# One more batch transposed by the DMA engines instead of TensorE, in an attention + ELU feed-forward kernel

## Chip, cores, metric

One core of one Trainium2 chip. The metric is device time in microseconds (us); a kernel is run several times, and what is told is the median of those runs with its lowest and highest. Every profile below is one execution of the kernel named. Its span is about 1.7 us shorter than the device time of the same run.

## The reference

Eight batches, eight heads, 576 positions, 64 numbers per head. Heads 0 to 3 see the last 32 positions (local), heads 4 to 7 see every 32nd position back (strided). The outputs become 4,608 tokens of 512 numbers, which go through two matrices with an ELU between them.

```python
scores = (1 / np.sqrt(D)) * np.matmul(q, k.transpose(0, 1, 3, 2))
rel = pos[:, None] - pos[None, :]
mask_local   = (rel >= 0) & (rel < 32)
mask_strided = (rel >= 0) & (pos[None, :] % 32 == pos[:, None] % 32)
attn = softmax(np.where(mask, scores, -1e9))
x = np.matmul(attn, v)                 # -> 4608 x 512
h = x @ w_in                           # -> 4608 x 2048   (layer 1)
g = np.where(h > 0, h, np.exp(np.minimum(h, 0)) - 1)
out = g @ w_out                        # -> 4608 x 512    (layer 2)
```

q, k and v are normal numbers times 0.1, so the scores are tiny and the softmax is nearly even over what the mask allows.

## The kernel before

TensorE multiplies nearly all of the time (busy 96% of the span). Layer 1 goes in tiles of 8 matmuls (128x256), layer 2 in steps of 4 (128x512), and the attention of later batches is fitted in between. Tokens go through in blocks of 256, which are numbered from 0.

The scores need q and k with the 64 numbers of a head on the partitions, so both are transposed after the load. There are two ways, and the kernel uses both. Batches 0, 1 and 2 use TensorE (`piece_T`), with a copy out of PSUM by VectorE or ScalarE; from batch 3 on, the DMA engines do it on their way from SBUF to SBUF (`dma_T`):

```python
    def dma_T(b, which):                       # issued by SP; 4 per batch
        i = b % 2
        out_, in_, n = {
            "qs": (qsT[i], qs.rearrange("p h c -> p (h c)"), RP),
            "ks": (ksT[i][:, 0:16 * RP], ks.rearrange("p h c -> p (h c)"), RP),
            ...                                # "ql", "kl": the local heads
        }[which]
        nc.sync.dma_start_transpose(out=out_.rearrange("p (c n) -> p c n", n=n), in_=in_)

    def piece_T(b, hp, engs=None, wide=True):
        ...
                nc.tensor.transpose(o, x, identity[0:n, 0:n])
        for i, (dst, blk) in enumerate(both):
            copy(engs[i] if engs else nc.vector, dst, ps[i])
```

There is one `qs` and one `ks` buffer for all batches, so the load of the next batch's strided q waits for the transpose of this one's. All loads from batch 1 on are issued by GpSimd, in the order of the program:

```python
    load_str(2, qs, q)                         # before the second attention loop
    load_str(2, ks, k)
    load_kl16(2)
    load_ql16(2)
    load_vl16(2)
    ...
    for it in ("2 S4 2 S5 2 2 B4 S6 2 E4 A5 S7 2 E5 B6 2 E6 A7 2 E7 v "
               "T0 2 S0 S1 2 T1 k B0 2 E0 S2 2 A1 E1 S3 2 B2 E2 2 A3 2 E3 t 2 x").split():
        # "2": a layer 2 step of blocks 0 and 1;  S, A/B, E: scores, value products, tail of batch 1
        # T: transposes of batch 1;  v: load of vs of batch 2;  k, x: loads of batch 3
        # t: piece_T of the strided heads of batch 2
    ...
    for p, n in ((0, 8), (1, 10)):             # the local heads of batch 2, between layer 1 tiles
        at(n, lambda p=p: do(("TT", 2, p)))
    for b in range(3, B):                      # st: the layer 1 tile of its first scores
        at(st - (3 if b == 3 else 4), lambda b=b: Ts(b))   # the four dma_T
    ...
        l2_to(n + 10)                          # layer 2 steps done before layer 1 tile n
```

The middle third of each value tile holds ones, so that one product gives a softmax sum along with the values; ScalarE writes them (`one_columns`), partly behind the first scores and partly after batch 0.

The softmax here doesn't subtract the row's maximum and nothing guards it: scores larger than these inputs give would overflow.

Of the kernel before, what the change touches and what calls it, by code (L numbers as in the profile page):

```python
# [17 lines left out]
D = 64  # L18
HG = 4
NS = 8  # L20
# [10 lines left out]
def kernel(  # L31
# [46 lines left out]
    qlb = [const([RP, 2, NS, 2 * D], BF16, f"qlb{i}") for i in range(2)]  # L78
    qld = [t.rearrange("p a s c -> p (a s c)").rearrange("p (h c) -> p h c", h=HG) for t in qlb]
    klb = [const([LQ, 2, LB, 2 * D], BF16, f"klb{i}") for i in range(2)]  # L80
# [32 lines left out]
    def load_ql16(b):  # L113
        if b < 3:
            nc.gpsimd.dma_start(out=qld[b % 2][0:RS],
                                in_=q[b, 0:HG].rearrange("h (p s) d -> p h (s d)", s=NS))
            return
        for h in range(HG):
            nc.gpsimd.dma_start(  # L119
                out=qlb[b % 2][0:RS, h // 2, :, (h % 2) * D:(h % 2 + 1) * D],  # L120
                in_=q[b, h].rearrange("(p s) d -> p s d", s=NS))
# [59 lines left out]
    dist = const([RS, RS], I32, "dist")  # L181
    nc.vector.memset(warm, 1.0)  # L182
    nc.vector.memset(identity, 1.0)
    nc.vector.memset(base_l, 1.0)
    for t in (qs, ks):
# [3 lines left out]
        base=0, pattern=[[1, 128]], channel_multiplier=-1,  # L189
    )  # L190
    load_str(0, qs, q)
    load_str(0, ks, k)
# [40 lines left out]
    def pitch(b):  # L233
        return RS if b < 3 else RP

    def t_parts(b, hp, nm):
        i, a, n = b % 2, hp % 2, RS
        if hp >= 2:
            src = qs if nm == "q" else ks
            dst = (qsT if nm == "q" else ksT)[i][:, a * 8 * n:(a + 1) * 8 * n]  # L240
            blk = [src[0:n, 2 * a + j // 4, (j % 4) * 128:(j % 4 + 1) * 128] for j in range(8)]
        elif nm == "q":
            dst = qlT[i][:, a * 8 * n:(a + 1) * 8 * n]
            blk = ([qlb[i][0:n, a, j] for j in range(NS)] if b not in (1, 2) else
                   [[qld[i][0:n, 2 * a + x, j * D:(j + 1) * D] for x in range(2)]
                    for j in range(NS)])
        else:
            dst = klT[i][:, PRE + a * S:PRE + (a + 1) * S]
            blk = [klb[i][:, a, j] for j in range(LB)]
        return dst, blk  # L250
# [4 lines left out]
    def piece_T(b, hp, engs=None, wide=True):  # L255
# [6 lines left out]
        for i, (dst, blk) in enumerate(both):  # L262
            n = S // len(blk)
            for j, x in enumerate(blk):
                o = ps[i][:, j * n:(j + 1) * n]
                if type(x) is list:
                    for z in range(2):
                        nc.tensor.transpose(o[z * D:(z + 1) * D], x[z], identity[0:n, 0:n])
                else:
                    nc.tensor.transpose(o, x, identity[0:n, 0:n])  # L270
        for i, (dst, blk) in enumerate(both):
# [252 lines left out]
    P = [(p, u) for p in range(4) for u in range(2)]  # L524
    def one_columns(i):
        for t in (vlx[i], vsx[i]):
            o = t.rearrange("p a t (y d) -> p (a t) y d", d=D)[:, :, 1, :]
            nc.scalar.copy(o, warm[0:o.shape[0], 0:D].unsqueeze(1).to_broadcast(o.shape))  # L528

    for it in ("f7 S0 S1 1 f6 T1 f6 S2 S3 m f8 T2 T3q T3k f3 S4 S5 f3 S6 S7 M4 f3 E4 M5 f3 E5 M6 f3 E6 "  # L530
               "v M7 f3 E7 M0 f3 E0 M1 f3 E1 M2 f3 E2 M3 f12 E3").split():
# [3 lines left out]
        elif it[0] == "f":  # L535
            spins(n)
        elif it == "1":
            one_columns(0)
        elif it == "v":
# [17 lines left out]
    nc.vector.memset(qlb[1][64:RP], 0.0)  # L557
    nc.vector.memset(vlx[1][0:PRE, :, 0, :], 0.0)
    one_columns(1)
    load_str(1, qs, q)  # L560
# [23 lines left out]
    load_str(2, ks, k)  # L584
    load_kl16(2)
    load_ql16(2)
    load_vl16(2)

# [12 lines left out]

    for it in ("2 S4 2 S5 2 2 B4 S6 2 E4 A5 S7 2 E5 B6 2 E6 A7 2 E7 v "
               "T0 2 S0 S1 2 T1 k B0 2 E0 S2 2 A1 E1 S3 2 B2 E2 2 A3 2 E3 t 2 x").split():
        n = int(it[-1]) if it[-1].isdigit() else 0
        if it == "2":
            l2_to(l2n[0] + 1)
        elif it == "v":
            load_str(2, vs, v)
        elif it == "k":
            load_kl16(3)  # L610
            load_ql16(3)
            load_vsx16(3)
        elif it == "t":
            for p in (2, 3):
                piece_T(2, p)
        elif it == "x":
            load_str(3, qs, q)
            load_str(3, ks, k)
            load_vl16(3)
        elif it[0] == "T":  # L620
            piece_T(1, n, (nc.vector, nc.scalar))
        elif it[0] in "AB":
# [8 lines left out]

    def Ts(b):
        for w in ("qs", "ks", "kl", "ql"):
            dma_T(b, w)


    SC = {2: (2.5, 5.5, 9, 12), }
    SC.update({b: tuple(15 + 16 * (b - 3) + 4 * i for i in range(4)) for b in range(3, B)})
    for p, n in ((0, 8), (1, 10)):
        at(n, lambda p=p: do(("TT", 2, p)))  # L640

    for b in range(3, B):
        st = int(SC[b][0])
        if b > 3:
            at(st - 13, lambda b=b: (load_str(b, qs, q), load_str(b, ks, k), load_kl16(b),
                                     load_ql16(b), load_vsx16(b), load_vl16(b)))
        at(st - (3 if b == 3 else 4), lambda b=b: Ts(b))
    for b in range(2, B):
# [7 lines left out]
    for n, (j, t) in enumerate(L1S):  # L656
        for f in jobs.pop(n, []):
            f()
        l2_to(n + 10)
        for f in jobs.pop(n + .5, []):  # L660
# [33 lines left out]
```

## Time and profile before

| | before |
|---|---|
| device time | 324.3 us (324.25 to 324.75, 3 runs); beside the changed kernel 324.52 (324.25 to 324.92, 4 runs) |
| profiled span | 322.6 us |
| TensorE busy | 310.8 us, 96% |
| mean granted clock of TensorE | 0.999 |

How to read a line of the timeline: start, length, engine, source line, operation, output<-input, shape, how many, and in brackets the idle time before it with what ended it. The main lines are shown in the prediction. Two more views: SP's and GpSimd's timelines around the first DMA transposes, those of batch 3, with the busy and DMA figures of that stretch (columns as in the prediction's stretches).

```profile
87.31 1.47 SPq L169 DMA_TRANSPOSE qsT<-qs  x1
88.89 1.88 SPq L169 DMA_TRANSPOSE ksT<-ks  x1
```

```profile
94.19 0.72 POOL L143 DMA_DIRECT2D ks<-in_k_dram  x1 [0.52 <-issue]
```

```profile
87.00:94.00 7.00, 7.00 (x67) 4.48 (x66) 4.69 (x10) 5.19 (x11) 0.75 (x1) 1.00 1.00 168
```

The lengths in SP's lines are SP's issuing, not the transfer: in the changed kernel SP's line for ksT of batch 2 ends at 62.94 us, and TensorE waits for that transpose until 68.56. The transfer shows in its user: the load of the next ks overwrites what the transpose reads, and goes at 94.19, 5.3 us after that transpose's issue, so the transpose took at most that. The DMA share (last column but one) is 1.00. (The DMA share adds up the times of all packets that start in the stretch and divides by the time of 16 engines; it comes out over 1 in places.)

### The profile page before, as it was taken

The numbers are of one execution on the slowest core, as the hardware profiler recorded it, in microseconds if no ns is written. First come the engines' busy times: TensorE is split into PE (matmuls) and PEld (weight loads), VectorE is DVE, ScalarE is ACT, GpSimd is POOL, SyncE is SP. The second block draws the span as 40 slices with busy tenths as digits, with TensorE's granted clock in tenths as the row PEclk, the third lists the DMA queues.
The fourth block names the chain that finished last, engine by engine and source line by source line (L and its number), as shares of the span: only waits on it lengthen the run. The fifth ranks groups of instructions, "written<-read, shape, count | busy, mean of one in ns | idle before, by whom it ended". The sixth has DMA issues, their size and how long they took to land.

```text
span 322.6 us, 7819 instructions
## 1 busy us (share of the span) xinstructions
PE 310.8 (96%) x2992; PEld 223.6 (69%) x2992; DVE 239.5 (74%) x485; ACT 220.2 (68%) x429; POOL 115.6 (36%) x162
## 2 busy tenths in 40 slices
PE   7898998989999999999999999999999999999994
PEld 5658953577667777777777777777777777777763
DVE  7664973477667888888888988898888866666660
ACT  3697766677688888777777777778888643443431
POOL 6352368788046903790259125920000000000000
PEclk9999999999999999999999999999999999999999
DMA  8999999999499949993999599969211111111112
GB/s 160 191 205 207 208 151 142 153 147 129 52 143 182 122 70 155 172 141 64 137 158 161 70 136 167 149 77 169 57 35 35 34 35 33 34 35 49 51 33 65
DMA packets 113990, 36.36 MB, mean 113 GB/s; under 512 B 101154, under 2 KB 107458, under 8 KB 113954
## 3 DMA queue, kind: packets, MB, share of 16 engines
q0 software_dynamic: 79696, 18.87, 61.3%
q1 hardware_dynamic: 32766, 16.28, 24.6%
q10 hardware_dynamic: 1492, 0.74, 1.0%
q8 instruction: 23, 0.38, 0.5%
q14 instruction: 13, 0.11, 0.1%
HBM read 38.04 MB, written 9.44 MB: 147 GB/s over the span
## 4 chain that ended last, share of the span: by engine, by line
PE 83%; DVE 6%; ACT 5%; DMA 3%; issue 1%; SPq 0%; DVEq 0%; ACTq 0%
PE ops L463 36%; PE hps L406 33%; PE sc L293 4%; PE ox L345 3%; DVE g L421 2%; DMA kl<-in_k_dram 2%; DMA ksT<-ks 1%; PE idle L487 1%; DVE g L440 1%; PE opl L478 1%; PE tp L270 1%; DVE he L420 1%; ACT vsx L528 1%; ACT big L437 1%; ACT e L296 1%
## 5 line engine op out<-in xcount | busy, mean ns | idle before, releaser
L463 PE MATMUL ops<-w_out_sb,g 128*128 128x512 bf16 x560 | 143.6, 380 | 0.1
L406 PE MATMUL hps<-xT,w_in_sb 128*128 128x256 bf16 x1088 | 140.7, 273 | 1.3 <-DVE g L421 1.3
L406 PEld LDWEIGHTS <-w_in_sb 128*128 128x128 bf16 x1088 | 117.3, 114 | 23.6 <-issue 1.5
L413 ACT ACTIVATE he<-hps 128x512 f32<-128x512 f32 x136 | 80.2, 593 | 52.3 <-PE hps L406 50.0
L421 DVE TENSOR_TENSOR g<-he,hps 128x512 bf16<-128x512 bf16 x130 | 89.4, 687 | 13.6
L463 PEld LDWEIGHTS <-g 128*128 128x128 bf16 x560 | 50.4, 98 | 37.2 <-DVE g L421 0.3
L420 DVE TENSOR_SCALAR he<-he 128x512 bf16<-128x512 f32 x130 | 57.7, 444 | 20.9 <-ACT he L413 19.5
L296 ACT ACTIVATE e<-sc 128x576 bf16<-128x576 f32 (+1 forms) x64 | 38.5, 645 | 4.6 <-PE sc L293 4.6
L468 ACT COPY osb<-ops 128x512 f32<-128x512 f32 x35 | 20.5, 587 | 12.3 <-PE ops L463 9.4
L143 POOL DMA_DIRECT2D qs<-in_q_dram x8 | 6.2, 774 | 48.9 <-DMA qsT<-qs 47.5
L348 ACT ACTIVATE ln<-ox 64x288 f32<-64x288 f32 x40 | 16.3, 409 | 10.7 <-PE ox L345 10.1
L125 POOL DMA_DIRECT2D klb<-in_k_dram x28 | 20.7, 747 | 7.9 <-DMA w_in_sb<-in_moe_w_in_dram 5.2
L133 POOL DMA_DIRECT2D vlx<-in_v_dram x28 | 21.9, 782 | 4.1 <-DMA w_out_sb<-in_moe_w_out_dram 1.9
L313 DVE TENSOR_TENSOR xT<-ox,rc 64x288 bf16<-64x288 f32 x40 | 18.1, 453 | 5.7 <-ACT rc L351 5.4
L317 DVE TENSOR_TENSOR xT<-ox,rc 64x288 bf16<-64x288 f32 x40 | 18.1, 453 | 5.5 <-ACT rc L351 5.1
L119 POOL DMA_DIRECT2D qlb<-in_q_dram x20 | 16.6, 833 | 13.8 <-DMA ks<-in_k_dram 10.0
L134 POOL DMA_DIRECT2D vlx<-in_v_dram x28 | 17.3, 618 | 4.2 <-DMA qlb<-in_q_dram 2.1
L351 ACT ACTIVATE rc<-ln 128x288 f32<-128x288 f32 x40 | 17.7, 443 | 1.3
L138 POOL DMA_DIRECT2D vsx<-in_v_dram x20 | 16.2, 816 | 0.9 <-DMA klb<-in_k_dram 0.9
L349 ACT ACTIVATE ln<-ox 64x288 f32<-64x288 f32 x40 | 16.1, 403 | 0.5
L304 DVE TENSOR_TENSOR pm<-e,mask_l 128x576 bf16<-128x576 bf16 x32 | 13.5, 453 | 3.3 <-ACT e L296 3.0
L487 PE MATMUL idle<-warm 128*128 128x256 bf16 x92 | 14.3, 299 | 1.3 <-DVE warm L182 1.3
(101 smaller groups left out, 243.2 us busy)
## 6 DMA issues: line engine op xcount, KB each, us to landing
out_dram<-osb SPq DMA_DIRECT2D x31, 144.0 KB
qs<-in_q_dram POOLq DMA_DIRECT2D x8, 288.0 KB, 6.4
ks<-in_k_dram POOLq DMA_DIRECT2D x8, 288.0 KB, 8.7
w_in_sb<-in_moe_w_in_dram POOLq DMA_DIRECT2D x2, 1024.0 KB, 17.0
w_out_sb<-in_moe_w_out_dram POOLq DMA_DIRECT2D x4, 512.0 KB, 15.7
klb<-in_k_dram POOLq DMA_DIRECT2D x28, 72.0 KB, 8.2
vlx<-in_v_dram POOLq DMA_DIRECT2D x28, 72.0 KB, 3.6
qlb<-in_q_dram POOLq DMA_DIRECT2D x20, 72.0 KB, 7.0
```

The source lines that it names most:

```text
L125: nc.gpsimd.dma_start(out=klb[b % 2][:, h // 2, :, (h % 2) * D:(h % 2 + 1) * D], in_=k[b, h].rearrange("(t p) d -> p t d", p=LQ))
L133: nc.gpsimd.dma_start(out=t[PRE:128], in_=x)
L296: nc.scalar.activation(e[0:R], sc[0:R, :, 0:W], ACT.Exp, scale=scale)
L313: nc.vector.tensor_mul(xs[:, u * W:(u + 1) * W], o[pr], rc[pr])
L317: nc.vector.tensor_mul(dst, o[pr].rearrange(pat, b=3, s=NS), rc[pr].rearrange(pat, b=3, s=NS))
L351: nc.scalar.activation(rc, ln, ACT.Exp, scale=-1.0)
L406: nc.tensor.matmul(hps[:, mm], lhsT=w_in_of(m, c), rhs=xT[:, c, r0:r0 + SUB], start=(c == 0), stop=(c == KC - 1))
L413: nc.scalar.activation(e, hps, ACT.Exp)
L420: eng.tensor_scalar(e1, e, scalar1=1.0, scalar2=1.0, op0=ALU.min, op1=ALU.subtract)
L421: nc.vector.tensor_tensor(gt, e1, hps, op=ALU.max)
L463: nc.tensor.matmul(ops, lhsT=g[:, m, kk * 128:(kk + 1) * 128], rhs=w_out_sb[:, m, :], start=(m == 0), stop=(m == MC - 1))
L468: nc.scalar.copy(o_sb, ops)
```

## The change

The intent: take the last transposes that TensorE can be spared (batch 2) off it, fill two idle places of TensorE with layer 2 steps, and take a hold-up of ScalarE and VectorE at 25 to 31 us away by writing the constants at the start. Its core:

```diff
@@ load_ql16: q of batches 1, 2 strided, like later batches @@
-        if b < 3:
-            nc.gpsimd.dma_start(out=qld[b % 2][0:RS],
-                                in_=q[b, 0:HG].rearrange("h (p s) d -> p h (s d)", s=NS))
-            return
@@ constants, right after the first memset @@
     nc.vector.memset(warm, 1.0)
+    nc.vector.memset(vlx[1][0:PRE, :, 0, :], 0.0)
...
+    for i in range(2):
+        one_columns(i)                 # was: behind the first scores, and after batch 0
@@ pitch @@
-        return RS if b < 3 else RP
+        return RS if b < 2 else RP
@@ second attention loop @@
-    for it in ("2 S4 2 S5 2 2 B4 S6 2 E4 A5 S7 2 E5 B6 2 E6 A7 2 E7 v "
-               "T0 2 S0 S1 2 T1 k B0 2 E0 S2 2 A1 E1 S3 2 B2 E2 2 A3 2 E3 t 2 x").split():
+    for it in ("2 S4 2 S5 2 2 B4 S6 2 E4 A5 S7 2 E5 B6 2 E6 A7 v 2 t E7 T0 2 S0 S1 2 T1 k B0 2 E0 S2 2 A1 E1 S3 t B2 2 "
+               "E2 A3 E3 x").split():
         elif it == "v":
             load_str(2, vs, v)
+            load_kl16(2)               # these three stood ahead of vs
+            load_ql16(2)
+            load_vl16(2)
         elif it == "k":
+            load_str(3, qs, q)         # these two stood at "x"
+            load_str(3, ks, k)
+            load_vsx16(3)
             load_kl16(3)
             load_ql16(3)
-            load_vsx16(3)
         elif it == "t":
-            for p in (2, 3):
-                piece_T(2, p)
+            Ts(2, *(("qs", "ks") if l2n[0] < 10 else ("kl", "ql")))
...
-    for p, n in ((0, 8), (1, 10)):
-        at(n, lambda p=p: do(("TT", 2, p)))
...
-        at(st - (3 if b == 3 else 4), lambda b=b: Ts(b))
+        at(st - 4, lambda b=b: Ts(b, "qs", "ks"))
+        at(st - (0 if b == 3 else 4), lambda b=b: Ts(b, "kl", "ql"))
...
-        l2_to(n + 10)
+        l2_to(max(n + 10, min(13 + (n + 2) // 2, 16)))
```

Left out: the strided branch of `piece_T` that q of batches 1 and 2 no longer needs, and piece T0's second copy, which goes from ScalarE to VectorE.

More of the change, by code (lines that the diff above doesn't have):

```diff
@@ L78 @@
     qlb = [const([RP, 2, NS, 2 * D], BF16, f"qlb{i}") for i in range(2)]
-    qld = [t.rearrange("p a s c -> p (a s c)").rearrange("p (h c) -> p h c", h=HG) for t in qlb]
     klb = [const([LQ, 2, LB, 2 * D], BF16, f"klb{i}") for i in range(2)]
@@ L190, with one_columns @@
     )
+    def one_columns(i):
+        for t in (vlx[i], vsx[i]):
+            o = t.rearrange("p a t (y d) -> p (a t) y d", d=D)[:, :, 1, :]
+            nc.scalar.copy(o, warm[0:o.shape[0], 0:D].unsqueeze(1).to_broadcast(o.shape))
+    for i in range(2):
+        one_columns(i)
     load_str(0, qs, q)
@@ L243, in t_parts @@
             dst = qlT[i][:, a * 8 * n:(a + 1) * 8 * n]
-            blk = ([qlb[i][0:n, a, j] for j in range(NS)] if b not in (1, 2) else
-                   [[qld[i][0:n, 2 * a + x, j * D:(j + 1) * D] for x in range(2)]
-                    for j in range(NS)])
+            blk = [qlb[i][0:n, a, j] for j in range(NS)]
         else:
@@ L265, in piece_T @@
                 o = ps[i][:, j * n:(j + 1) * n]
-                if type(x) is list:
-                    for z in range(2):
-                        nc.tensor.transpose(o[z * D:(z + 1) * D], x[z], identity[0:n, 0:n])
-                else:
-                    nc.tensor.transpose(o, x, identity[0:n, 0:n])
+                nc.tensor.transpose(o, x, identity[0:n, 0:n])
         for i, (dst, blk) in enumerate(both):
@@ L524 @@
     P = [(p, u) for p in range(4) for u in range(2)]
-    def one_columns(i):
-        for t in (vlx[i], vsx[i]):
-            o = t.rearrange("p a t (y d) -> p (a t) y d", d=D)[:, :, 1, :]
-            nc.scalar.copy(o, warm[0:o.shape[0], 0:D].unsqueeze(1).to_broadcast(o.shape))
-    for it in ("f7 S0 S1 1 f6 T1 f6 S2 S3 m f8 T2 T3q T3k f3 S4 S5 f3 S6 S7 M4 f3 E4 M5 f3 E5 M6 f3 E6 "
+    for it in ("f7 S0 S1 f6 T1 f6 S2 S3 m f8 T2 T3q T3k f3 S4 S5 f3 S6 S7 M4 f3 E4 M5 f3 E5 M6 f3 E6 "
                "v M7 f3 E7 M0 f3 E0 M1 f3 E1 M2 f3 E2 M3 f12 E3").split():
@@ L536 @@
             spins(n)
-        elif it == "1":
-            one_columns(0)
         elif it == "v":
@@ L557 @@
     nc.vector.memset(qlb[1][64:RP], 0.0)
-    nc.vector.memset(vlx[1][0:PRE, :, 0, :], 0.0)
-    one_columns(1)
     load_str(1, qs, q)
@@ L584 @@
     load_str(2, ks, k)
-    load_kl16(2)
-    load_ql16(2)
-    load_vl16(2)
     L2S = [(j, kk, part) for j in range(NSUB) for kk in range(2) for part in range(4)]
@@ L600, in l2_to, with Ts @@
             l2n[0] += 1
-    for it in ("2 S4 2 S5 2 2 B4 S6 2 E4 A5 S7 2 E5 B6 2 E6 A7 2 E7 v "
-               "T0 2 S0 S1 2 T1 k B0 2 E0 S2 2 A1 E1 S3 2 B2 E2 2 A3 2 E3 t 2 x").split():
+    def Ts(b, *names):
+        for w in names:
+            dma_T(b, w)
+    for it in ("2 S4 2 S5 2 2 B4 S6 2 E4 A5 S7 2 E5 B6 2 E6 A7 v 2 t E7 T0 2 S0 S1 2 T1 k B0 2 E0 S2 2 A1 E1 S3 t B2 2 "
+               "E2 A3 E3 x").split():
         n = int(it[-1]) if it[-1].isdigit() else 0
@@ L608 @@
             load_str(2, vs, v)
+            load_kl16(2)
+            load_ql16(2)
+            load_vl16(2)
         elif it == "k":
+            load_str(3, qs, q)
+            load_str(3, ks, k)
+            load_vsx16(3)
             load_kl16(3)
             load_ql16(3)
-            load_vsx16(3)
         elif it == "t":
-            for p in (2, 3):
-                piece_T(2, p)
+            Ts(2, *(("qs", "ks") if l2n[0] < 10 else ("kl", "ql")))
         elif it == "x":
-            load_str(3, qs, q)
-            load_str(3, ks, k)
             load_vl16(3)
         elif it[0] == "T":
-            piece_T(1, n, (nc.vector, nc.scalar))
+            piece_T(1, n, (nc.vector, nc.scalar if n else nc.vector))
         elif it[0] in "AB":
@@ L630, in at @@
         jobs.setdefault(int(2 * n) / 2, []).extend(its)
-    def Ts(b):
-        for w in ("qs", "ks", "kl", "ql"):
-            dma_T(b, w)
     SC = {2: (2.5, 5.5, 9, 12), }
     SC.update({b: tuple(15 + 16 * (b - 3) + 4 * i for i in range(4)) for b in range(3, B)})
-    for p, n in ((0, 8), (1, 10)):
-        at(n, lambda p=p: do(("TT", 2, p)))
     for b in range(3, B):
```

## The prediction

Passages that told of the hardware what no trace of this case shows are cut from the recorded text, and the places are marked. The 5.5 us and the 1.5 to 1.9 us for a transpose were read from the trace of the kernel before. The 0.1 us "for a switch of shape" is an estimate; in the chain of the kernel before a layer 2 step takes 0.97 us behind scores (at 81.49) and 0.86 behind a layer 1 tile (at 91.31). Both kernels give the DMA transposes 80 rows where 72 hold data (`RP` and `RS`).

> **What bounds the kernel now.** Names used below: qs and ks are the tiles of the strided heads' q and k, ql and kl of the local heads'; with T they are the transposed ones; a layer 2 step is four 128x512 matmuls into one accumulator. I read the page first, busy shares and slices, then TensorE's waits, then the chain of waits and TensorE's timeline where those waits lie.
>
> ```profile
> PE 310.8 (96%) x2992; PEld 223.6 (69%) x2992; DVE 239.5 (74%) x485; ACT 220.2 (68%) x429; POOL 115.6 (36%) x162
> ...
> PE   7898998989999999999999999999999999999994
> ...
> DMA  8999999999499949993999599969211111111112
> ...
> 0.00:20.00 20.00, 16.52 (x224) 11.85 (x224) 13.84 (x39) 12.12 (x21) 8.72 (x16) 1.00 1.02 180
> 20.00:40.00 20.00, 18.67 (x203) 16.60 (x203) 13.29 (x24) 15.04 (x25) 9.12 (x14) 1.00 1.14 209
> 40.00:60.00 20.00, 18.52 (x217) 9.79 (x216) 11.37 (x24) 13.18 (x26) 14.40 (x21) 1.00 1.48 157
> 60.00:80.00 20.00, 18.82 (x239) 13.30 (x238) 13.48 (x30) 15.24 (x32) 16.90 (x23) 1.00 1.45 134
> 80.00:100.00 20.00, 19.80 (x212) 13.33 (x211) 13.47 (x28) 14.77 (x29) 7.18 (x11) 1.00 0.85 110
> ```
>
> In the last five lines the columns are stretch, length, busy us of PE, PEld, DVE, ACT, POOL, clock, DMA share, GB/s. TensorE is the bound: from 80 us to the last slice it hardly idles. So a microsecond gained before 80 us moves the end by one, provided no new wait takes it back. Two things can be gained: TensorE work (3.0 us of transposes, below) and idle time, 1.3, 1.5 and 1.2 us in the second to fourth stretch (20 minus the first busy number). The 3.5 us in the first are the loads and latency at the start.
>
> Who causes the idle time:
>
> ```profile
> PE hps L406 <- DVE g L421: 1.3, 1, 1.3
> PE sc L293 <- ACT klT L253: 1.3, 1, 1.3
> ...
> PE so L368 <- DVE pm L298: 1.1, 1, 1.1
> ...
> ```
>
> The columns are total us, times, longest. The first lies at 31.2 us, the second at 53.7, the third at 70.8. The chain shows what is behind the first:
>
> ```profile
> 25.15 0.91 DVE qlb L557
> ...
> 27.14 1.04 ACT vsx L528
> 28.18 0.92 ACT big L437
> ...
> 30.04 1.23 DVE g L440
> ...
> 32.49 1.03 PE hps L406 x8
> ```
>
> A memset of 0.91 us on VectorE and one of 0.22 behind it hold back ScalarE's copies of ones into v's second buffers; behind those stands the first exponential of layer 1, whose matmuls were done at 26.7. VectorE starts 1.4 us late, and a TensorE buffer comes free late.
>
> [...] the first of batch 3 is issued at 87.31 us and the load it holds up goes at 92.92, with a DMA share of 0.2 just before; SP takes 1.5 to 1.9 us for each, so 80x2048 bf16 (0.33 MB) every 1.9 us is at most 172 GB/s. I use 5.5 us from issue to landing.
> [...] GpSimd stands 47.5 us in four waits on the transposes of qs. So the order in a queue decides when a transfer starts.
> [...] Here one record lasts 197 ns, but they are pipelined:
>
> ```profile
> 63.85 0.43 PE L270 MATMUL tp<-identity,qs 72*128 72x72 bf16 x8
> ...
> 64.77 0.42 PE L270 MATMUL tp<-identity,ks 72*128 72x72 bf16 x8
> 65.03 1.03 PE L463 MATMUL ops<-w_out_sb,g 128*128 128x512 bf16 x4
> ```
>
> 32 of them hold TensorE from 63.85 to 65.03, 1.18 us, 37 ns each.
>
> **The change part by part.**
> *Transposes of batch 2 off TensorE.* The strided pieces free 1.18 us. The two local ones begin at 78.44 and 83.62; each delays what follows by some 0.77 us (0.65 to the next group, and about 0.1 for a switch of shape). Sum 1.18 + 2 x 0.77 = 2.7 us on the bound engine, all of it path. VectorE loses 8 copies of 0.45 us; only the 0.2 us wait on klT at 81.19 is on the path.
> *Batch 1.* With q strided in the load, its two pieces need 8 transposes of 128 columns, not 16 of 64: 0.38 us becomes about 0.26, twice, 0.24 us. The k copy of piece 0 moves from ScalarE (0.64) to VectorE (0.45) and ends about 0.2 us earlier; that path sets the wait at 53.7.
> *Ones and a memset to the start.* The 1.3 us wait at 31.2 goes. The price: four copies on ScalarE, which back to back took 0.72 and 0.95 here, so 2 x 1.67 = 3.35 us; ScalarE is free from 2.08 (table load) to 6.07 (k lands). They fit with 0.6 us to spare. The 0.22 us memset stands in front of the memsets of qs and ks, which the first strided loads wait for: at most 0.2 us lost. Net gain 1.1 us.
> *Layer 2 steps moved.* The second attention loop has 13 rather than 16 steps; the other three come in the first five layer 1 tiles. Walking the timeline, 13 steps leave TensorE waiting before the last value product of batch 1 (pm 0.5 us late) and again before the first layer 1 tile of the next block: logarithm 0.41, exponential 0.44 and multiply 0.46, about 1.5 us with the handovers, less one step of 0.97, 0.6 us. Given back: the 1.05 us at 70.8 and some 0.35 in smaller gaps around it, now filled by steps. Net gain 0.3 us.
> *Loads.* q of batches 1 and 2 becomes 4 issues of 0.83 us for one of 0.74, some 2.6 us more of GpSimd each. The strided pieces drain well: k of batch 1, 576 runs each, landed at 43.5, 43.9, 44.4 and 44.8, while the contiguous q, 288 long runs, landed 2.0 us later. Since GpSimd keeps 8 DMAs in flight (its k issue at 29.89 goes as the weight load eight DMAs back lands, 10.1 + 19.5 = 29.6, and the next six go by the same rule), I place qs and ks of batch 2 at 49.1 and 49.9. Their latencies then:
>
> ```profile
> L143 POOL DMA_DIRECT2D ks<-in_k_dram x1: 722/722/722, 48.6 to 48.6; - x1
> DMA to landing us min/median/max: 6.3/6.3/6.3
> ```
>
> So ks lands at 56.2, SP takes 1.9 us, and 5 us after its issue, about 61, ksT is there. The first scores of batch 2 stand at 67.74 now and at about 65 after the gains. That is 4 us of room. kl and ql have over 8 us. Nothing on the path.
>
> Sum: 2.7 + 0.24 + 0.2 + 0.2 + 1.1 + 0.3 = 4.7 us; 324.3 - 4.7 = 319.6 us, 1.5% less.
>
> **The rivals.**
> *Transposes late.* If the crowded DMA engines (share 1.5 between 40 and 80 us[...]) stretch a transpose to 9 us or more, TensorE waits at the first scores of batch 2 and takes 1 to 3 us back: 320.5 to 322.5. For it: the change adds four transposes of over 1,200 packets each and 4,032 packets of q in the fullest stretch; ksT already held up scores twice, 0.7 us in total. Against it: the 4 us of room, and from 48 to 52 us the share is only 1.0, because GpSimd's issue and not the engines limits the flow. I give it 25%.
> *Batch 3 pushed back.* Its loads go out behind those of batch 2, its strided ones behind the transposes. In the kernel before they landed by 80 us for transposes at 87 to 93; now about 75 to 86. Its local transposes are moved three tiles later, and their use is 16 us on. Would cost 1 us; 10%.
> *The layer 2 shift buys nothing.* VectorE feeds both stretches; if filling the gap at 70.8 only reopens it before tile 0, the end is 320 or a little over; 25%. If instead pm comes in time, 319.
> *Start collides.* If ScalarE is late for the cast of k at 6.07, the whole start shifts by up to 1 us: 320.5; 10%.
> *More than counted.* If every gap between 40 and 80 us closes (2.7 us), the result is near 317.5. Against it: the wait before the scores at 53.7 hangs on ScalarE's eviction of layer 2 and VectorE's copies, which the change hardly touches.
>
> **Range and chances.** Transposes and the early wait (about 4 us) are nearly certain; the rest runs from -2.5 to +1.7. Predicted 319.6 us, 8 in 10 within 318.0 to 321.8. Over 2% faster means under 317.8, which needs the last rival: 0.08. Slower by 2% would need 11 us of new waits: 0.01. Within 2%: 0.91.
>
> **What would show it.** TensorE: no transposes after 60 us, 92 fewer in number. Its waits: no 1.3 us at layer 1 near 31 us; the wait on klT near 53 still over 0.8 us; the wait of 1.1 us on pm near 70 gone, and a new one of 0.3 to 0.8 us at the first layer 1 tile after batch 1. ScalarE's copies of ones done before 6.0 us. No wait of TensorE's weight loads on ksT<-ks before 80 us; if one over 0.5 us stands there, the first rival holds. The offset of the two timelines should be 1.1 to 1.4 us at the first layer 2 step, about 3.5 at the first layer 1 tile of block 2 (65.90 now; three layer 2 steps short), and 4.5 to 5 from 90 us on. If the offset shrinks again after 90 us, my claim that the rest is bound by TensorE alone is wrong.

## The result

The changed kernel took 325.64 us (325.28 to 326.29, 4 runs) against 324.52 us for the kernel before in the same rounds. The ratio is 1.0036, with a 95% interval of 1.0015 to 1.0056. Executions over 1.5% slower than the fastest of the same kernel are left out of the means. A ratio is always the mean time of one kernel's fast runs over the mean of the other's of the same rounds, so it is not quite the ratio of the medians. The class "within 2%" is right. The time is not: 319.6 was predicted, with 318.0 to 321.8 as the range, and 325.64 lies outside it. Not 1.5% was gained, but 0.4% lost.

Source lines differ by a few between the kernels: L290, L403, L460 here are L293, L406, L463 before. First the page of the changed kernel: busy shares, slices of TensorE, of its clock and of the DMA engines.

```profile
PE 306.6 (95%) x2856; PEld 222.2 (69%) x2900; DVE 237.8 (73%) x478; ACT 219.5 (68%) x428; POOL 120.2 (37%) x168
...
PE   7899998869999899999999999999999999999995
...
PEclk9999999979999999999999999999999999999998
DMA  7999999999999999993999599939211111111212
```

PEld has 2,900 records where before had 2,992: the 92 fewer that were predicted. But the ninth slice (64.8 to 72.9 us) has a 6 for TensorE and a 7 for its clock, and the DMA engines, which showed a 4 at 81 to 89 and at 113 to 121 us before, show a 9 there. TensorE's waits name the rest (total us, times, longest):

```profile
PE sc L290 <- DMA ksT<-ks: 3.1, 1, 3.1
PE sc L290 <- DVE klT L254: 1.4, 2, 1.0
...
PE sc L290 <- DMA qlT<-qlb: 1.0, 1, 1.0
...
PE so L371 <- DVE pm L301: 0.5, 1, 0.5
...
PE hps L403 <- DVE xT L314: 0.4, 1, 0.4
```

Against the three lines of the prediction: the 1.3 us on g and the 1.1 us on pm are gone, the wait on klT has stayed (1.0), and the two small ones foreseen are there (0.55 and 0.40 against 0.5 and 0.6). New are two waits on transposes. Where the first lies, in TensorE's timeline:

```profile
64.47 1.03 PE L460 MATMUL ops<-w_out_sb,g 128*128 128x512 bf16 x4
68.56 0.30 PE L290 MATMUL sc<-qsT,ksT 64*128 64x72 bf16 x8 [3.07 <-DMA ksT<-ks]
...
70.30 1.90 PE L403 MATMUL hps<-xT,w_in_sb 128*128 128x256 bf16 x8
```

TensorE is ready for the first scores of batch 2 at 65.5 us (the prediction said about 65) and starts them at 68.56. Two things are to be seen. Behind the wait, a layer 1 tile of 8 matmuls takes 1.90 us where such a tile takes 1.06; the stretches of 2 us say why. Their last columns are clock, DMA share and GB/s:

```profile
60.00:80.00 20.00, 15.48 (x156) 10.61 (x158) 10.82 (x22) 12.79 (x27) 12.43 (x18) 0.91 1.65 162
...
68.00:70.00 2.00, 1.44 (x19) 1.04 (x21) 0.41 (x1) 0.65 (x1) 1.36 (x3) 0.89 2.04 193
70.00:72.00 2.00, 2.00 (x17) 1.24 (x16) 1.26 (x4) 1.13 (x2) 1.85 (x3) 0.50 1.42 117
72.00:74.00 2.00, 1.74 (x20) 0.98 (x21) 0.92 (x2) 1.74 (x4) 2.00 (x4) 0.75 1.90 194
```

The granted clock is 0.50 from 70 to 72 us and lower than 1 in the stretches on both sides; in stretches of half a microsecond it is at or near 0.50 from about 69.6 to 73.0, some 3.4 us. The second thing is the cause of the wait, in the chain of waits (start, length, what) and in SP's timeline:

```profile
56.41 0.64 PE ops L460 x3
57.05 11.47 DMA ksT<-ks
...
68.56 0.30 PE sc L290 x8
...
100.97 11.87 DMA qlT<-qlb
...
112.98 0.43 PE sc L290 x12
```

```profile
54.74 2.19 SPq L164 DMA_TRANSPOSE qsT<-qs  x1
57.05 5.89 SPq L164 DMA_TRANSPOSE ksT<-ks  x1
...
97.11 3.64 SPq L164 DMA_TRANSPOSE klT<-klb  x1
100.97 4.20 SPq L164 DMA_TRANSPOSE qlT<-qlb  x1
```

The transpose of ks is issued at 57.05 and has landed 11.5 us later, where the same transpose of batch 3 had taken at most 5.3 in the kernel before. Even its issuing takes SP 5.89 us instead of 1.88. The same is seen at qlT of batch 3, which the change issues three layer 1 tiles later than before: 11.9 us in flight, and a wait of 1.02 us.

To see where the time goes, I compared the start of the same layer 1 weight load in both profiles, counted from the start (after minus before; my own derivation from the two timelines):

| place (time in before) | offset, us | predicted |
|---|---|---|
| first layer 1 tile (24.8) | +0.28 | at most +0.2 |
| first layer 2 steps (33 to 41) | -0.82 | -1.1 to -1.4 |
| first tile of block 2 (65.7) | -3.73 | about -3.5 |
| after the first scores of batch 2 (68.0) | +0.82 | |
| after the slow clock (74.7) | +1.99 | |
| from 85.6 on | +0.27 | -4.5 to -5 |
| after the wait on qlT (114.8) | +1.36 | -4.5 to -5 |
| last tile (312) | +1.58 | -4.7 |

So the walk came true, within 0.3 to 0.5 us, up to 66 us. What is lost is lost at two waits on transposes, and in the slow clock behind the first.

### The profile page after: what moved, and what is told of

Read it like the earlier page. It is cut to its first block, busy times and chain, and to the rows that moved or that the text cites. A ratio compares the mean times of both kernels' runs of the same rounds, so it can differ in the third digit from the quotient of the medians.

```text
span 324.0 us, 7606 instructions
## 1 busy us (share of the span) xinstructions
PE 306.6 (95%) x2856; PEld 222.2 (69%) x2900; DVE 237.8 (73%) x478; ACT 219.5 (68%) x428; POOL 120.2 (37%) x168
## 3 DMA queue, kind: packets, MB, share of 16 engines
q1 hardware_dynamic: 37886, 17.56, 28.6%
## 4 chain that ended last, share of the span: by engine, by line
PE 77%; DMA 11%; DVE 5%; ACT 3%; issue 2%; POOL 0%; SPq 0%; DVEq 0%; ACTq 0%
PE ops L460 32%; PE hps L403 32%; DMA ksT<-ks 5%; DMA qlT<-qlb 4%; PE sc L290 3%; PE ox L342 3%; DMA ks<-in_k_dram 3%; PE idle L484 1%; DVE g L437 1%; PE hpw L428 1%; DVE g L418 1%; PE opl L475 1%; DVE he L417 1%; DVE xT L310 1%; PE o_ps L375 1%
## 5 line engine op out<-in xcount | busy, mean ns | idle before, releaser
L403 PE MATMUL hps<-xT,w_in_sb 128*128 128x256 bf16 x1088 | 141.8, 274 | 0.9 <-DVE xT L314 0.4
L460 PE MATMUL ops<-w_out_sb,g 128*128 128x512 bf16 x516 | 137.2, 380 | 2.6 <-issue 0.6
L403 PEld LDWEIGHTS <-w_in_sb 128*128 128x128 bf16 x1088 | 117.6, 114 | 23.5 <-issue 0.9
L460 PEld LDWEIGHTS <-g 128*128 128x128 bf16 x560 | 50.5, 98 | 37.5 <-issue 0.5
L293 ACT ACTIVATE e<-sc 128x576 bf16<-128x576 f32 (+1 forms) x64 | 38.5, 645 | 11.4 <-PE sc L290 11.4
L114 POOL DMA_DIRECT2D qlb<-in_q_dram x28 | 23.1, 830 | 16.7 <-DMA ks<-in_k_dram 8.2
L295 DVE TENSOR_TENSOR pm<-e,mask_s 72x576 bf16<-72x576 bf16 x32 | 13.5, 449 | 5.3 <-ACT e L293 5.1
```

What stands on the lines that cost most here:

```text
L114: nc.gpsimd.dma_start(out=qlb[b % 2][0:RS, h // 2, :, (h % 2) * D:(h % 2 + 1) * D], in_=q[b, h].rearrange("(p s) d -> p s d", s=NS))
L293: nc.scalar.activation(e[0:R], sc[0:R, :, 0:W], ACT.Exp, scale=scale)
L403: nc.tensor.matmul(hps[:, mm], lhsT=w_in_of(m, c), rhs=xT[:, c, r0:r0 + SUB], start=(c == 0), stop=(c == KC - 1))
L460: nc.tensor.matmul(ops, lhsT=g[:, m, kk * 128:(kk + 1) * 128], rhs=w_out_sb[:, m, :], start=(m == 0), stop=(m == MC - 1))
```

## The experiments

The theory after reading: the transposes of batch 2 share the DMA engines with the loads of batch 2 (vs, kl, ql, vl) and are stretched by them. The gap of 3 us then drops the clock (to 0.50 above), which adds to the cost. Rivals: (a) the short runs of the strided q load are what stretches them; (b) only the long runs of vs do; (c) the lower clock has another cause than the wait; (d) the parts were mis-sized anyway, and the wait only covers that up. Session by session, the kernel before had medians of 324.86 (first four experiments), 324.60 (next four) and 324.61 to 324.64 us (the last six, on a chip with more scatter: one run of the kernel before took 333.89). Unless said otherwise, all runs are correct.

### e1_const: only the constants, on the kernel before

```diff
+    nc.vector.memset(vlx[1][0:PRE, :, 0, :], 0.0)      # behind the first memset
+    for i in range(2):
+        one_columns(i)                                 # ahead of the first strided loads
-        elif it == "1": one_columns(0)
-    nc.vector.memset(vlx[1][0:PRE, :, 0, :], 0.0)      # after batch 0
-    one_columns(1)
```

> One part alone: the kernel before, with only the constants of v set at the very beginning. Theory (each part's gain arrives, and one transpose that lands late eats them): the wait of 1.3 us near 31 us shrinks to about 0.2 and the start is some 0.3 us longer, as in the changed kernel, so about 0.8 us less than before, ratio near 0.9975. Rival (the constants at the start cost as much as they bring, by delaying the first loads): no change or slower, ratio 1.000 or over.

Measured: 323.44 us (322.58 to 324.91, 6 runs), ratio 0.9963 [0.9937, 0.9988]. TensorE's waits, and the place in its timeline:

```profile
PE so L376 <- DVE pm L306: 1.6, 2, 1.3
```

```profile
30.75 1.03 PE L414 MATMUL hps<-xT,w_in_sb 128*128 128x256 bf16 x8 [0.29 <-DVE g L429]
```

The wait of 1.3 us at layer 1 is 0.29, and the wait on pm near 70 us stays, as it should. About 1.2 us of gain (0.37% of 324.9; the interval allows 0.4 to 2.0) against 1.1 in the prediction: this step holds by itself.

### e2_pe_str: the change, but qs and ks of batch 2 on TensorE again

```diff
-            Ts(2, *(("qs", "ks") if l2n[0] < 10 else ("kl", "ql")))
+            Ts(2, "kl", "ql")
...  # ahead of "x":
+            for p in (2, 3):
+                piece_T(2, p)
+            load_str(3, qs, q)         # no longer at "k"
+            load_str(3, ks, k)
```

(The pitch of qsT and ksT is 72 again for this batch.)

> The changed kernel with one part undone: qs and ks of batch 2 transposed on TensorE again, in 32 steps before the first layer 1 tile of block 2; ql and kl stay with the DMA. Theory: the wait of 3.1 us on ksT near 66 us and the halved clock after it (70 to 74 us) go, 1.2 us of TensorE work comes back, partly in the 0.4 us wait before that tile: some 3.3 to 4 us less than the changed kernel, about 322 us, ratio to before near 0.993. Rival (the loss is from the moved layer 2 steps, and the wait only shows where it becomes visible): no gain over the changed kernel, ratio 1.003.

Measured: 322.39 us (321.61 to 323.83, 6 runs), ratio 0.9935 [0.991, 0.9959]. No wait on ksT of batch 2 is left; the transposes themselves wait for VectorE (0.8 us). The whole change without the one late pair is 0.65% faster than before, so the loss sits in that pair, and rival (d) is refuted in its strong form.

One more thing is needed further down. TensorE idles 0.55 us before these 32 transposes and 0.84 us amid them, and the clock (last column but two) stays:

```profile
62.00:64.00 2.00, 1.72 (x24) 1.26 (x24) 1.78 (x5) 0.00 (x0) 2.00 (x4) 1.00 1.58 185
64.00:66.00 2.00, 2.00 (x18) 1.69 (x16) 0.15 (x1) 1.26 (x3) 2.00 (x4) 1.00 1.47 139
```

### e3_alone: the loads of kl, ql, vl behind the transposes

```diff
         elif it == "v":
             load_str(2, vs, v)
-            load_kl16(2); load_ql16(2); load_vl16(2)
         elif it == "k":
             load_str(3, qs, q); load_str(3, ks, k)     # these wait for the transposes
+            load_kl16(2); load_ql16(2); load_vl16(2)
```

> The changed kernel with the loads of kl, ql and vl of batch 2 behind the transposes of qs and ks in GpSimd's queue, so that these two run nearly alone. Theory (the transposes are slow because many short pieces of loads share the engines): ksT lands 5 to 6 us after its issue at 57 us instead of 11.5, no wait or under 0.5 us at the first scores of batch 2, clock stays at 1.0 there; kl and ql land later, so a new wait of 0 to 3 us may stand at the scores of the local heads. Rival (a transpose of 80 rows issued right behind another takes that long whatever runs beside it): still over 9 us and a wait of 2 us or more.

Measured: 325.75 us (322.59 to 326.88, 4 runs), ratio 1.001 [0.9961, 1.006]. TensorE's timeline at the first scores (they have no wait in front), the load that overwrites ks, and TensorE's waits:

```profile
64.81 0.30 PE L290 MATMUL sc<-qsT,ksT 64*128 64x72 bf16 x8
```

```profile
63.91 0.70 POOL L138 DMA_DIRECT2D ks<-in_k_dram  x1 [0.45 <-issue]
```

```profile
PE sc L290 <- DMA ksT<-ks: 2.4, 1, 2.4
PE sc L290 <- DMA qlT<-qlb: 2.3, 1, 2.3
```

No wait and no slow tile at the first scores: ksT, issued at 56.56, is there by 63.91, when the load that overwrites its source goes: at most 7.4 us, with vs beside it (issued at 50.67, as in the changed kernel, where it landed at 60.5). (GpSimd itself was busy just before, so whether it was the expected 5 to 6 us can't be said.) So vs by itself does not bring a transpose to 11.5 us, and rival (b) falls here. But the loads that made room are now late themselves. qlT of batch 2 is waited for at 79.6 us, and batch 3's ksT (the wait of 2.4 us) at 95.8. The offset goes from -2.3 to +1.8 there, with slow matmuls again behind the wait: a layer 2 step takes 1.80 us and a tile 1.92, where they take 1.04 and 1.06 (the mean clock of this run is 0.995). So ksT is in time when kl, ql and vl are not beside it; this order is no repair.

### e13_clear: all four loads of batch 2 behind the transposes

```diff
         elif it == "v":
-            load_str(2, vs, v); load_kl16(2); load_ql16(2); load_vl16(2)
+            pass
         elif it == "k":
             load_str(3, qs, q); load_str(3, ks, k)
+            load_str(2, vs, v); load_kl16(2); load_ql16(2); load_vl16(2)
```

> The changed kernel with all four loads of batch 2 that followed qs and ks (vs, kl, ql, vl) behind the two transposes in GpSimd's queue. Theory (the loads beside it stretch a transpose): ksT lands 4 to 6 us after its issue, that is by 62 to 63 us, and TensorE has no wait on it at the first scores of batch 2; the loads moved come late and cost new waits of several us on vs and on the local heads of batch 2, so the kernel as a whole is slower than the changed one. Rival (two transposes in a row on this queue take 10 us by themselves): ksT lands at 66 us or later.

Measured: 327.03 and 328.71 us (2 runs), ratio 1.009 [1.0026, 1.0155]. GpSimd's timeline (the load that overwrites ks), and the busy stretch while the transposes run, here and in the changed kernel:

```profile
61.92 0.70 POOL L138 DMA_DIRECT2D ks<-in_k_dram  x1 [0.40 <-issue]
```

```profile
57.00:62.00 5.00, 4.45 (x50) 2.24 (x49) 2.29 (x5) 4.54 (x12) 0.79 (x2) 1.00 1.06 162
```

```profile
57.00:62.00 5.00, 4.40 (x49) 2.29 (x49) 2.29 (x5) 4.54 (x12) 1.44 (x2) 1.00 1.91 174
```

The first two fences are this experiment, the third is the changed kernel. With no load beside it, ksT goes from its issue at 56.59 to landing in at most 5.3 us, the same bound as for batch 3, at a DMA share of 1.06. In the changed kernel the share over the same 5 us is 1.91 and the engines move hardly more (174 against 162 GB/s). The traces' DMA records, which the views do not list one by one, say the same when the changed kernel is set against batch 3's transposes in the kernel before: there 3,506 packets of 256 bytes start in the 7 us from 87 to 94, 501 a us, and in the changed kernel 894 in these 5 us, 179 a us. (They are the transposes': in the kernel before none starts between 8 and 87 us.) This is the prediction's 61 us (61.9 here), had the traffic been absent. The price of the moved loads is again higher than the gain: a wait of 2.0 us on vs and one of 3.35 on batch 3's ksT.

### e4_early: the loads of qs, ks ahead of batch 1's v, the transposes four layer 2 steps earlier

```diff
     load_ql16(1)
-    load_vl16(1)
...
     load_str(2, qs, q)
     load_str(2, ks, k)
+    load_vl16(1)
...
-    for it in ("2 S4 2 S5 2 2 B4 ... A7 v 2 t E7 ...
+    for it in ("2 S4 2 S5 2 2 t B4 ... A7 v 2 E7 ...
```

> The changed kernel with qs and ks of batch 2 loaded ahead of vl of batch 1 and their transposes four layer 2 steps sooner in SP's queue. Theory: the issue of ksT moves from 57 to about 52 us, and even with 11.5 us in flight it lands by 64, before TensorE asks at 65.5: no wait, no clock drop, some 4 us less than the changed kernel, 321 to 321.8 us, ratio to before 0.989 to 0.992. Rival (the DMA engines are full, so an earlier place only moves the lateness to another load, such as vl of batch 1): waits of 2 us or more elsewhere before 80 us and a ratio of 1.0 or over.

Measured: 321.20 us (320.63 to 322.42, 6 runs), ratio 0.9898 [0.9874, 0.9922]. SP's timeline and TensorE's waits:

```profile
51.71 2.53 SPq L164 DMA_TRANSPOSE ksT<-ks  x1
```

```profile
PE sc L290 <- DMA qlT<-qlb: 1.2, 1, 1.2
```

The wait on ksT is gone, the clock stays up (0.998 in the mean), and the offset to the kernel before is -4.37 us from 86 us on, where the prediction had said -4.5 to -5. Then the second wait, on batch 3's qlT, takes 1.2 back, and the profile ends at -3.3. So the prediction's sum was nearly right for a kernel whose transposes come in time.

### e5_spin: idle matmuls in the gap

```diff
+    def busy(n):
+        t = p_x.tile([128, 2, 512], F32, tag="x", name="busy")
+        for _ in range(n):
+            spin(t[:, 0, 0:256])
+    at(2.5, lambda: busy(29))          # ahead of the first scores of batch 2
```

> The changed kernel with 29 idle matmuls (some 3.1 us) in front of the first scores of batch 2, where TensorE stands waiting for ksT. Theory (the 3 us of standing still also halves the granted clock for some 4 us afterwards, worth about 1.4 us): the transposes land as late as before, at about 68.5 us, but the clock stays at 1.0, the layer 1 tile after it takes 1.0 us and not 1.9, and the kernel is 1.2 to 1.6 us faster than the changed one, 324 to 324.5 us, ratio to before 0.998 to 1.000. Rival (the slow matmuls after the wait are slow for another reason, such as late operands): ratio 1.003 to 1.005 as for the changed kernel, and the tile stays slow.

Measured: 324.03 us (322.99 to 324.85, 6 runs), ratio 0.9978 [0.9951, 1.0004]; the mean clock is 0.999 or 1.000 in every run. TensorE's timeline:

```profile
64.95 3.33 PE L484 MATMUL busy<-warm 128*128 128x256 bf16 x29
68.78 0.30 PE L290 MATMUL sc<-qsT,ksT 64*128 64x72 bf16 x8 [0.50 <-DMA ksT<-ks]
...
70.25 1.06 PE L403 MATMUL hps<-xT,w_in_sb 128*128 128x256 bf16 x8
```

The scores start as late as before (68.78), but the tile that had taken 1.90 us takes 1.06. Filling the gap with useless work gains 1.6 us (325.64 to 324.03, across sessions; 0.58 points by the ratios). So rival (c) falls: the gap lowered the clock, and the clock was about a third of what the late transpose cost.

### e8_qrun: q of batch 2 in long runs

```diff
+        if b == 2:                     # 288 long runs instead of 4 x 576 short ones
+            nc.gpsimd.dma_start(
+                out=qlb[0]... .rearrange("p (h c) -> p h c", h=HG)[0:RS],
+                in_=q[b, 0:HG].rearrange("h (p s) d -> p h (s d)", s=NS))
+            return
```

The layout is wrong: the transpose then mixes up the slices of local q in batch 2. The comparison with the reference passed all the same, presumably since scores this small leave the softmax nearly even; the result is not to be used.

> The changed kernel with q of the local heads of batch 2 loaded in long runs again, one transfer for four; the output is wrong on purpose, since the transpose then reads the old layout. Theory (the crowd of all loads in flight slows the transposes, the strided q is one part of it): ksT of batch 2 still takes 8 us or more and the wait at the first scores is 1 to 2.5 us. Rival (the strided q of this batch is what makes them late): ksT lands within 6 us and no wait is left. A third outcome, the wait as long as before (3 us), would say that long runs hold up a transpose as much as short ones.

Measured: 329.34 us (328.45 to 330.61, 4 runs), ratio 1.0142 [1.0106, 1.0177]:

```profile
71.79 0.42 PE L296 MATMUL sc<-qsT,ksT 64*128 64x72 bf16 x8 [6.78 <-DMA ksT<-ks]
```

Issued at 56.48, ksT now takes 15.3 us. Rival (a), as the only cause, falls: without the short runs of q the transpose takes longer still. Whether it is the long runs of q that hold it up more is not shown, because q now takes one place in GpSimd's queue and not four, and loads of vl move up: five are issued between 54.5 and 67.0 us here, where in the changed kernel the first goes at 63.57.

### e9_vs and e10_vs_b3: vs behind kl and ql

That led back to rival (b): keep the short runs, and issue only the long ones of vs later. e10_vs_b3 is the same with batch 3's local transposes issued as early as those of later batches.

```diff
         elif it == "v":
-            load_str(2, vs, v)
             load_kl16(2)
             load_ql16(2)
+            load_str(2, vs, v)
             load_vl16(2)
...  # e10_vs_b3 only
-        at(st - (0 if b == 3 else 4), lambda b=b: Ts(b, "kl", "ql"))
+        at(st - 4, lambda b=b: Ts(b, "kl", "ql"))
```

> The changed kernel with one load moved: vs of batch 2 (288 runs of 2 KB read, 1 KB written) goes out behind kl and ql of batch 2 and not ahead of them. Theory ([...] it is vs that makes ksT late): ksT lands by 65 us, the wait at the first scores of batch 2 is under 0.8 us and the clock stays, about 321.5 to 322.5 us, ratio 0.990 to 0.994. Rival (the number of packets in flight counts, whatever their length): the wait stays at 2 us or more and the ratio at 1.001 or over.

> The same with the transposes of kl and ql of batch 3 right behind those of its qs and ks. If both late transposes were all that stood between the prediction and the chip, this comes to the predicted sum: 319.6 to 320.5 us, ratio 0.985 to 0.988. If the shorter lead of the transposes still leaves a wait, 321 to 323.

e9_vs: 328.08 us in the median of all six; one run of the six took 1,163 us (the profiled one, so there is no usable profile), one was slow, and the four fast ones lie between 324.62 and 328.8: ratio 1.0062 [1.0007, 1.0117]. e10_vs_b3: 326.22 us (325.88 to 328.47, 6 runs), ratio 1.0056 [1.0015, 1.0096]. Both theories were missed; e9_vs fell where its rival had it (1.001 or over). In the timelines of e10_vs_b3, of GpSimd and of TensorE:

```profile
60.35 0.74 POOL L138 DMA_DIRECT2D vs<-in_v_dram  x1
```

```profile
69.61 0.30 PE L290 MATMUL sc<-qsT,ksT 64*128 64x72 bf16 x8 [4.05 <-DMA ksT<-ks]
```

ksT was issued at 59.34 and took 10.3 us, at a DMA share of 1.93. As a test of rival (b) this run is not clean: vs was not out of the way, it went 1.0 us behind ksT, GpSimd waited for its landing until 71.58, and loads of vl followed it. Cleaner is the changed kernel itself. There vs had landed at 60.5, and ksT needed 8.0 us more with only kl, ql and then vl in flight, in short packets: from 60.5 to 68.5 us 2,876 of 128 bytes and 853 of 4 start in their queue, and none longer. So short runs in number do it as well. Part of the longer wait here is that the transposes were issued some 2 us later than in the changed kernel.

Put together, the time of one and the same transpose (ks of batch 2, from issue to landing):

| beside it | us | from |
|---|---|---|
| no load | at most 5.3 | e13_clear |
| vs (issued at 50.67) | at most 7.4 | e3_alone |
| kl, ql in short runs, from 60.4 vs, then vl | 10.3 | e10_vs_b3 |
| vs (until 60.5), kl, ql in short runs, first of vl from 63.6 | 11.5 | the change |
| vs (until 60.2), kl in short runs, ql in long runs, vl from 54.5 | 15.3 | e8_qrun |

### e7_l2: only the layer 2 shift, on the kernel before

```diff
-               "T0 2 S0 S1 2 T1 k B0 2 E0 S2 2 A1 E1 S3 2 B2 E2 2 A3 2 E3 t 2 x").split():
+               "T0 2 S0 S1 2 T1 k B0 2 E0 S2 2 A1 E1 S3 B2 2 E2 A3 E3 t x").split():
...
-        l2_to(n + 10)
+        l2_to(max(n + 10, min(13 + (n + 2) // 2, 16)))
```

> One part alone: the kernel before with only the layer 2 steps moved later; TensorE still makes all transposes of batch 2, now right in front of the first layer 1 tile. The prediction's step gives it 0.3 us, plus up to 0.6 because the transposes now fill the wait before that tile: 323.5 to 324.3, ratio 0.996 to 0.999. Rival (the shift costs, because two new waits stand where steps were taken away): ratio 1.001 or more.

Measured: 325.73 us (324.38 to 326.54, 6 runs), ratio 1.0019 [0.9988, 1.0051]. Two runs with a clock of 1.000 took 324.38 and 324.55, the four with 0.993 to 0.995 took 325.53 to 326.54. TensorE's timeline of a run of the second sort, and its stretches:

```profile
63.78 0.42 PE L270 MATMUL tp<-identity,qs 72*128 72x72 bf16 x8 [0.84 <-DVE xT L317]
...
65.73 3.02 PE L406 MATMUL hps<-xT,w_in_sb 128*128 128x256 bf16 x16
```

```profile
64.00:66.00 2.00, 1.94 (x20) 1.01 (x18) 1.28 (x4) 0.00 (x0) 2.00 (x3) 0.65 1.68 156
66.00:68.00 2.00, 2.00 (x11) 1.45 (x10) 0.00 (x0) 0.32 (x1) 0.95 (x3) 0.50 2.15 136
```

In the two runs without a clock drop the shift gains nothing that shows against 324.60; with it, it loses about a microsecond or more. The drop comes after two idle times of only 0.55 and 0.84 us around the 32 TensorE transposes. But e2_pe_str has the same idle times around the same transposes, and its clock stayed at 1.00 (shown there); so they can be followed by a drop and need not be, and what decides is not shown. The result fits the rival "the layer 2 shift buys nothing", to which the prediction gave 25%; a gain of 0.3 us lies inside the interval.

### e6_both, e11_all, e12_l2old, e14_mix: putting it together

e6_both is e4_early plus batch 3's local transposes at their early place. e11_all is e6_both with vs behind kl and ql. e12_l2old is e6_both with the layer 2 order of the kernel before. e14_mix has 14 steps in the second loop and the other two in later layer 1 tiles.

```diff
# e6_both = e4_early and
-        at(st - (0 if b == 3 else 4), lambda b=b: Ts(b, "kl", "ql"))
+        at(st - 4, lambda b=b: Ts(b, "kl", "ql"))
# e12_l2old = e6_both and, with 16 steps in the loop,
-        l2_to(max(n + 10, min(13 + (n + 2) // 2, 16)))
+        l2_to(n + 10)
# e14_mix = e6_both and, with 14 steps in the loop,
+        l2_to(max(n + 10, min(15 + n // 4, 16)))
```

> The version with qs and ks of batch 2 early, and the transposes of kl and ql of batch 3 issued right behind those of its qs and ks, not four tiles later. Theory: the last wait on a transpose (1.2 us, qlT of batch 3, in flight during the loads of batch 4) goes or falls under 0.4 us, so about 1 us less than the early version, some 320.2 us, ratio to before 0.985 to 0.988. Rival (the loads of kl and ql of batch 3 land too late for that place, so SP stands and holds back the stores): no gain, ratio 0.989 to 0.992.

> Three orders changed in the changed kernel: qs and ks of batch 2 early, vs of batch 2 behind kl and ql, kl and ql of batch 3 transposed early. Against the version with the first and last of these (ratio 0.9872, one wait of 1.3 us on vl of batch 1 left in its profile): the wait on vl stays, since vs is not in flight then: 320 to 320.6, ratio 0.985 to 0.988. Rival (vs too held back those loads): ratio under 0.984.

> The version with early qs, ks of batch 2 and early transposes of batch 3, but with the layer 2 steps in the order of the kernel before. The shift alone measured nothing (1.0019 with an interval over 1), so theory: the same time as with the shift, within 0.5 us of 320.5, ratio 0.986 to 0.989; the waits at pm near 70 us come back and the ones before the first tile of block 2 go. Rival (the shift is worth its gain once the transposes are off TensorE): 1 us or more slower, ratio 0.990 or over.

> The version with early qs, ks of batch 2 and early kl, ql transposes of batch 3, with 14 layer 2 steps in the second attention loop, one of them before the value products that waited for vl of batch 1, and two in the next block. Theory: the waits on vl (1.3 us) and on pm before the last product (0.55) go, the one at pm near 70 us stays under 0.5: 319.5 to 320.3 us, ratio 0.984 to 0.987. Rival (the waits only change places): 320.4 to 321, ratio 0.987 to 0.989.

| | us (lowest to highest, 6 runs each) | ratio to before, 95% | offset at the end of the profile |
|---|---|---|---|
| e6_both | 320.52 (319.93 to 321.3) | 0.9872 [0.9847, 0.9896] | -3.7 |
| e11_all | 321.36 (320.39 to 322.29) | 0.9892 [0.9856, 0.9928] | |
| e12_l2old | 321.68 (319.85 to 323.88) | 0.9905 [0.9858, 0.9953] | -4.3 |
| e14_mix | 321.34 (319.17 to 323.98, the last slow) | 0.9905 [0.9858, 0.9952] | -5.1 |

e6_both has no wait on a DMA transpose left. One wait of its own is new: batch 1's v, pushed back by the earlier loads, comes 1.3 us late. TensorE's waits of e6_both:

```profile
PE o_ps L375 <- DMA vlx<-in_v_dram: 1.3, 1, 1.3
```

It beats both kernels: 1.3% under the kernel before, and by 5.1 us in the medians under the change as it was (325.64, in another session). e11_all missed its expectation: the wait on batch 1's v grew to 1.7 us and batch 3's ksT was waited for 0.9. e12_l2old has the pm wait of the old order back (1.1 us) and not the others. Its ratio lies where its rival had it (0.990 or over) and its fastest run, 319.85, below what its theory said; the interval covers both, and it is not told apart from e6_both. Alone or in company, the layer 2 shift is worth nothing that these runs resolve. e14_mix has the shortest single profile of all (span 317.5 us against 322.6 before), and the waits on vl and on the late pm are gone from it. But its ratio missed the range of both theory and rival, and in the noisier session its interval overlaps that of e6_both, so it is not shown to be better.

## Why the prediction was wrong, point by point

**The bound: right up to 112 us.** TensorE was the bound, and what was gained before 66 us moved everything after it, until a wait took it back. By the prediction's own sign ("if the offset shrinks again after 90 us") the claim that the rest hangs on TensorE alone failed at one place, the wait on qlT at 113 us.

**Transposes off TensorE, ones at the start: right as far as measured.** The first is not measured alone. It is contained in e4_early's -4.37 us by 86 us, against -4.5 to -5, where the prediction had 2.7 of 4.7 us for it. The second gained 1.2 us alone (1.1 predicted). In the changed kernel's profile the offset at the first layer 2 step was -0.82, about 0.3 less than expected, and it starts 0.28 us late. That start varies from run to run: of two runs on one chip whose code is the same up to there, e6_both starts 0.29 early and e5_spin 0.24 late. ScalarE's copies of ones were done at 5.55 us, so the rival "Start collides" did not come.

**The step that failed: "Loads", with "I use 5.5 us from issue to landing".** The prediction placed the landing of ksT at about 61 us with 4 us of room (its sum takes 5 us of flight, not the 5.5 that it named). TensorE was ready at 65.5, near the 65 foreseen, but ksT was issued at 57.05, 0.9 us later than 56.2, and then took 11.5 us. The term was mis-sized by 6 us because it was read from batch 3, where nothing else was in flight (a DMA share of 1.00 that was the transposes' own), and used in a stretch where vs, kl, ql and the first vl were in flight (1.91). e13_clear shows the other half: at the same place without these loads it is at most 5.3 us. The prediction also read from batch 1 that strided loads "drain well", because q in long runs landed 2.0 us after the last k; but that q had been issued 2.8 us after it (37.47 against 34.64), so the lines do not say this.

**The rival "Transposes late" named what happened, and was sized too small.** It gave 25% to "a transpose of 9 us or more" and put 1 to 3 us on it. The wait alone was 3.1. The clock drop behind it was not in the prediction at all: it cost some 1.4 us of offset in the profile (the step from +0.82 to +1.99, where e4_early goes from -2.84 to -3.12), and 1.6 by e5_spin. Together that is 4.5 us, of which 0.4 was caught up in later gaps: between 65.7 and 85.6 us the changed kernel's offset rises by 4.0 (-3.73 to +0.27), while that of e4_early, whose ksT is in time, falls by 0.1 (-4.26 to -4.37). One argument against the rival was wrong in kind: the DMA share of 1.0 between 48 and 52 us (GpSimd busy for 4.00 of these 4) said nothing of the stretch from 57 on, when the transposes really ran.

**"Batch 3 pushed back": it came, and in the size foreseen.** It was given 10% and 1 us. The wait on qlT was 1.02 us, and the offset rose from +0.28 to +1.36 there. e6_both shows it from the other side: with these transposes issued early, its offset stays at -3.65 over the place where e4_early's goes from -4.37 to -3.15. "Their use is 16 us on" was no comfort with 11.9 us in flight behind a late issue at 100.97.

**The layer 2 shift: not confirmed.** The waits moved as foreseen (1.1 gone, 0.55 and 0.40 new), but the net gain of 0.3 us was not found; it is too small for these runs to exclude.

**The sum.** From -4.7 predicted to +1.58 in the profile is 6.3 us: 4.1 for the late ksT with its clock drop (net of what was caught up), 1.1 for qlT, 0.3 for the layer 2 shift, 0.3 to 0.5 at the start. That leaves a few tenths, which I can't put down to anything.

**What stays open.** No run separates the number of DMAs in flight from the number of their packets as what stretches a transpose. Short runs do it (the changed kernel after 60.5 us); what long ones add is not separated. e9_vs has no usable profile. Why the clock drops in some runs of e7_l2 and not in others, nor in the profile of e2_pe_str, is not shown by any run. Why e14_mix's best runs do not show in its mean was not followed.

## What to carry to other kernels

Take the time of a transfer from a place where the same traffic is beside it; here a transpose that took at most 5.3 us with no load in flight took 10.3 to 15.3 beside loads of three tiles or more. When a change may make TensorE wait, look at the clock behind the wait too: here, behind the wait of 3.1 us, it was at or near 0.50 for some 3.4 us, which cost about half as much again (1.4 to 1.6 us). And when a change that "moves work elsewhere" disappoints, issue the moved work earlier, into a quieter stretch, before giving it up: that alone turned +0.4% into -1.3%.
